# Which queue carries the first transposes and weight slabs of a fused SiLU MLP, and when each is issued

## The chip, the cores and the metric

The kernel runs on one core of a Trainium2 chip. The core has a matrix engine (TensorE, PE in the profile, with its weight loads shown as PEld), three other compute engines (VectorE or DVE, ScalarE or ACT, GpSimd or POOL), and SyncE (SP), which here only issues DMAs. SyncE and ScalarE each own one DMA queue; both queues feed the same 16 DMA engines. The metric is the device time of one execution in microseconds; lower is better. A profile comes from one further execution, with its own time.

## What is computed

The reference is a two-layer perceptron without biases, in bf16, on 2048 tokens:

```python
B, S, D, F = 1, 2048, 640, 1728
def reference(x, w1, w2):
    h = jnp.einsum("bsd,df->bsf", x, w1)
    h = jax.nn.silu(h)
    return jnp.einsum("bsf,fd->bsd", h, w2)
```

## The kernel before

Both layers contract over the partition axis of SBUF, so x is needed with its 640 columns on partitions. The kernel gets it so by transposing DMAs from HBM: the tensor `xT` has five tiles of 128 columns (index k, "tile k" below, DT = 5), each holding all 2048 tokens. `turned(c0, c1, k0, k1)` (lines 89 to 94) issues on SyncE one such DMA for tokens c0 to c1 and tiles k0 to k1. The first layer's weights are in `w1s`, again five slabs k of 128 rows; `slab(eng, k, f0, f1)` (line 118) loads the feature tiles f0 to f1 of slab k on the queue of `eng`. Every such DMA has a semaphore of its own, which stands at 16 once it has landed; `load` and `turned` return it as a point that an engine can be made to wait for.

The tokens go in four chunks of 512 (SCH). The first chunk is done in a special order, the opening: since weights and inputs arrive slab by slab, TensorE takes slab k=0 for eight feature tiles (NO = 8, one PSUM bank each), then k=1 for the same eight, and so on to k=4, after which ScalarE applies SiLU and writes `hT`. One feature tile of one k is a pair of matmuls (`step`, line 179), each with 64 of the 128 weight columns and 512 tokens, that run side by side. `sweep(k, ...)` waits for slab k and tile k and issues the eight pairs. Remaining feature tiles and chunks follow with all five k in a row, then the second layer, whose results are stored by SyncE, and the last of them by ScalarE too.

Before the first real matmul TensorE runs dummies on a zeroed tile `z` (`dummies`, line 129; `first_dummies`, line 135): thirteen matmuls of 128 weight columns and 256 columns of zeros, and then one pair with 64 weight columns each. They write PSUM bank 3, which the opening then starts anew.

A program begins with a barrier of all engines. `early(emit, engine, arrived)` (line 98) moves the instructions that `emit` makes ahead of it: for SyncE, ScalarE and VectorE (`arrived=False`) ahead of the engine's own arrival at the barrier, so that the barrier opens for nobody before these are issued; for TensorE (the opening, k = 0 to 2) behind its arrival but ahead of its wait. What follows in program order on an engine (SyncE's further loads, ScalarE's table load for SiLU at line 153, TensorE's k=3 and on) comes after the barrier.

Each engine's queue is in program order. The DMAs ahead of the barrier are issued before the change as follows:

| queue | order of issue before |
|---|---|
| SyncE | tiles 0 and 1; slab 0, feature tiles 5 to 7 (`ld_w1b`); slab 1; slab 2; tile 2; slab 3; tiles 3 and 4; slab 4 |
| ScalarE | slab 0, feature tiles 0 to 4 (NA = 5) |

After the barrier SyncE issues the rest of `w1s` (two DMAs), the fifteen one-tile transposes of chunks 1 to 3 (line 159) and `w2`.

What TensorE waits for in the opening: k=0 for `ld_t[0]` and `ld_w1[0]`, its sixth feature tile for `ld_w1b`, and each later k for `ld_w1[k]` and `ld_t[k]`. Where two names hold the same point, the second wait is left out by `wait` (line 63).

Of the kernel before, what the change touches and what calls it, by code (L numbers as in the profile page):

```python
# [9 lines left out]
def bass_standalone__dense_activation_silu__prompt_kernel(  # L10
# [13 lines left out]
    P = 128  # L24
    NB = 8
    BANK = 512
    DT = D // P
    FT = F // P
    FL = F - FT * P
    SCH = 512  # L30
    HB = 256
# [7 lines left out]
    pe, act, dve, pool, sp = nc.tensor, nc.scalar, nc.vector, nc.gpsimd, nc.sync  # L39

    with ExitStack() as es:
        def sb(name, shape, dtype):
            return es.enter_context(nc.sbuf_tensor(name, shape, dtype))
# [10 lines left out]
        z = sb("z", [P, HB], bf16)  # L54
        ps = es.enter_context(nc.psum_tensor("ps", [P, NB, BANK], fp32))
# [4 lines left out]
        def sem(name):  # L60
            s = es.enter_context(nc.semaphore(name))
            count[s.name if hasattr(s, "name") else name] = 0
            return [s, 0]

        def tick(ins, s, n=1):
            ins.then_inc(s[0], n)
            s[1] += n
            return (s, s[1])

        def wait(eng, *points):  # L70
            for pt in points:
                if pt is None:
                    continue
                s, v = pt
                key = (id(eng), id(s))
                if seen.get(key, 0) < v:
                    eng.wait_ge(s[0], v)
                    seen[key] = v

        s_pe, s_act, s_dve = sem("s_pe"), sem("s_act"), sem("s_dve")  # L80
# [4 lines left out]
        def load(eng, out_ap, in_ap):  # L85
            s = sem(f"s_ld{n_dma[0]}")
            n_dma[0] += 1
            return tick(eng.dma_start(out=out_ap, in_=in_ap), s, 16)

        def turned(c0, c1, k0, k1):  # L90
            s = sem(f"s_tr{n_dma[0]}")
            n_dma[0] += 1
            return tick(sp.dma_start_transpose(
                out=xT[:, k0:k1, c0:c1], in_=xf[c0:c1, k0 * P:k1 * P]), s, 16)

        ET = mybir.EngineType

        def early(emit, engine, arrived=True):
            n = len(nc.main_func.blocks[0].instructions)
            r = emit()  # L100
            lst = nc.main_func.blocks[0].instructions
            new = lst[n:]
            del lst[n:]
            at = next(
                i for i, ins in enumerate(lst)
                if ins.opcode == ("EventSemaphore" if arrived else "Drain") and ins.engine == engine
            )
            lst[at:at] = new
            return r
# [4 lines left out]
        NO = NB  # L114
        NA = 5
        CO = NO * P

        def slab(eng, k, f0=0, f1=NO):
            return load(eng, w1s[:, k, f0 * P:f1 * P], w1_v[:, k, f0 * P:f1 * P])

        ld_w1 = {}
        ld_t = {}
        ld_t[0] = ld_t[1] = early(lambda: turned(0, SCH, 0, 2), ET.SP, False)
        ld_w1[0] = early(lambda: slab(act, 0, 0, NA), ET.Activation, False)
        p_z = early(lambda: tick(dve.memset(z[:, :], 0.0), s_dve), ET.DVE, False)  # L125

# [2 lines left out]
        def dummies(n, w):  # L129
            for _ in range(n):  # L130
                for c0 in range(0, P, w):
                    pe.matmul(ps[c0:c0 + w, 3, 0:HB], lhsT=z[:, 0:w], rhs=z[:, :],  # L132
                              start=True, stop=True)

        def first_dummies():
            wait(pe, p_z)
            dummies(13, P)
            dummies(1, HC)

        p_warm = tick(pool.memset(warm[:, :], 0.0), s_pool)  # L140

        ld_w1b = early(lambda: slab(sp, 0, NA, NO), ET.SP, False)
        ld_w1[1] = early(lambda: slab(sp, 1), ET.SP, False)
        ld_w1[2] = early(lambda: slab(sp, 2), ET.SP, False)
        ld_t[2] = early(lambda: turned(0, SCH, 2, 3), ET.SP, False)
        ld_w1[3] = early(lambda: slab(sp, 3), ET.SP, False)
        ld_t[3] = ld_t[4] = early(lambda: turned(0, SCH, 3, DT), ET.SP, False)
        ld_w1[4] = early(lambda: slab(sp, 4), ET.SP, False)
        CM = CO + 2 * P
        ld_rest = load(sp, w1s[:, :, CO:CM], w1_v[:, :, CO:CM])  # L150
        ld_rest2 = load(sp, w1s[:, :, CM:F], w1_v[:, :, CM:F])
        wait(act, p_warm)
# [17 lines left out]
        def mm(o, l, r, start, stop, shared=False):  # L170
            return pe.matmul(o, lhsT=l, rhs=r, start=start, stop=stop, skip_group_check=shared)  # L171
# [7 lines left out]
        def step(b, k, ft, c0, c1, start=False, stop=False):  # L179
            for h0 in (0, HC):  # L180
                ins = mm(ps[h0:h0 + HC, b, :], w1s[:, k, ft * P + h0:ft * P + h0 + HC],
                         xT[:, k, c0:c1], start, stop, shared=True)
            return ins
# [9 lines left out]
        def opening():  # L193
            first_dummies()
            wait(pe, ld_t[0], ld_w1[0])
            for ft in range(NO):
                if ft == NA:
                    wait(pe, ld_w1b)
                part(0, ft, 0, SCH, start=True)
            for k in (1, 2):  # L200
                sweep(k, 0, SCH, ld_w1[k], ld_t[k])
# [11 lines left out]
        def bank():  # L213
            b = nxt[0] % NB
            nxt[0] += 1
            wait(pe, bank_free[b])
            return b

        wait(pe, ld_rest)
        for ft in range(NO, FT):  # L220
            b = bank()
            if ft == NO + 2:
                wait(pe, ld_rest2)
            for k in range(DT):
                ins = step(b, k, ft, 0, SCH, start=(k == 0), stop=(k == DT - 1))
            silu(hT[:, ft, 0:SCH], ps[:, b, :], b, tick(ins, s_pe))
        for c in range(1, NSC):
            wait(pe, ld_xc[c])
            for ft in range(FT):
                b = bank()  # L230
                for k in range(DT):
                    ins = step(b, k, ft, c * SCH, (c + 1) * SCH, start=(k == 0), stop=(k == DT - 1))
                h_last = silu(hT[:, ft, c * SCH:(c + 1) * SCH], ps[:, b, :], b, tick(ins, s_pe))
        h_tail = []
        for q in range(NSC // 2):
            b = bank()
            for k in range(DT):
                for hh in range(2):
                    c = 2 * q + hh
                    ins = mm(ps[hh * FL:(hh + 1) * FL, b, :], w1s[:, k, F0:F],  # L240
                             xT[:, k, c * SCH:(c + 1) * SCH],
                             start=(k == 0), stop=(k == DT - 1), shared=True)
# [133 lines left out]
        for u, eng in ((A, dve), (B, act), (C, act), (E, dve), (G2, act)):  # L376
            for ft in range(FT):
                ins = u.whole(ft, ft == FT - 1)
# [31 lines left out]
```

## Time and profile before

| what | value |
|---|---|
| median of three runs | 124.61 us (124.58, 124.61, 125.4) |
| the profiled execution's own time | 124.91 us |
| its span, first to last instruction | 123.4 us |
| TensorE busy in the span | 121.1 us, 98% |
| ScalarE, VectorE busy | 38.8 us, 7.0 us |
| dummies (line 132) | 15 matmuls, 3.3 us |
| first-layer matmuls (line 171, from xT and w1s) | 540, 59.2 us, 382 ns mean |
| DMA: bytes moved, mean rate | 10.42 MB, 84 GB/s |

The span runs from the first to the last instruction; the run's time also has what lies around it, 1.5 us here. A matmul's 382 ns is its time from start to end; the two of a pair and the pairs among themselves overlap, so the pace is read from starts, not from this. A DMA issue shows on the queue of its engine as SPq or ACTq; its length there is the time to issue, and "to landing" counts from the start of the issue to the last of its semaphore's sixteen steps. Times in the timeline are microseconds from the start of the span. In the windows view each column is an engine's busy time with the number of its instructions, and the last columns are the granted clock, the DMA engines' mean busy share (over 1 where packets of an engine overlap) and their rate.

### The profile page before, as it was taken

The page shows a single profiled execution, that of the slowest core. Times are in us where ns is not written, and L with a number is a line of the kernel's source. Part 1 is how long each engine was busy: PE and PEld are TensorE (multiplying, and loading weights), DVE is VectorE, ACT ScalarE, POOL GpSimd, SP SyncE. Part 2 cuts the span into 40 slices and gives each one's busy share as a digit, 9 for nine tenths or more (in the row PEclk, how much of TensorE's full clock was granted, in tenths as well). Part 3 has the DMA queues.
Part 4 walks back from the last instruction along what each step waited for, and adds up shares of the span by engine and source line. Part 5 has one row for each costly group of instructions (what it writes and reads, how often), then busy time and mean ns, then how long its engine had stood idle before and what let it go on. Part 6 is the DMA issues. An engine that isn't in the chain of part 4 may idle for free.

```text
span 123.4 us, 2299 instructions
## 1 busy us (share of the span) xinstructions
PE 121.1 (98%) x1057; PEld 59.5 (48%) x1057; DVE 7.0 (6%) x11; ACT 38.8 (31%) x67; POOL 0.3 (0%) x5
## 2 busy tenths in 40 slices
PE   8999999999999999999999999999999999999993
PEld 5455555555555555555544444444444444444452
DVE  0000000000000000000000022002201300222001
ACT  0041985555555555555530011001101200110110
POOL 0000000000000000000000000000000000000000
PEclk9999999999999999999999999999999999999999
DMA  6999945475992000000000005202200220022112
GB/s 142 234 271 302 157 103 108 94 75 92 288 391 70 0 0 0 8 0 0 0 0 5 0 5 115 56 0 106 106 0 5 106 106 0 5 106 106 53 74 86
DMA packets 19482, 10.42 MB, mean 84 GB/s; under 512 B 13457, under 2 KB 18961, under 8 KB 19473
## 3 DMA queue, kind: packets, MB, share of 16 engines
q1 hardware_dynamic: 19184, 10.05, 32.1%
q10 hardware_dynamic: 288, 0.23, 0.8%
q8 instruction: 8, 0.13, 0.5%
q14 instruction: 2, 0.01, 0.0%
HBM read 4.51 MB, written 2.62 MB: 58 GB/s over the span
## 4 chain that ended last, share of the span: by engine, by line
PE 95%; DMA 3%; ACT 0%; issue 0%
PE ps L171 95%; DMA xT<-in_x_dram 3%; ACT o_sb L254 0%
## 5 line engine op out<-in xcount | busy, mean ns | idle before, releaser
L171 PE MATMUL ps<-xT,w1s 128*64 128x512 bf16 x540 | 59.2, 382 | 0.1
L171 PE MATMUL ps<-w2s,hT 64*128 64x512 bf16 (+3 forms) x377 | 46.2, 369 | 0.0
L171 PEld LDWEIGHTS ps<-xT,w1s 128*64 128x64 bf16 x540 | 30.5, 111 | 28.6 <-issue 0.9
L175 ACT ACTIVATE hT<-ps 128x512 bf16<-128x512 f32 x52 | 30.0, 607 | 22.9 <-PE ps L171 22.9
L171 PEld LDWEIGHTS ps<-w2s,hT 64*128 64x128 bf16 (+1 forms) x377 | 21.0, 95 | 24.1 <-issue 0.2
L254 ACT CAST o_sb<-ps 128x512 bf16<-128x512 f32 (+1 forms) x9 | 5.0, 551 | 41.5 <-PE ps L171 41.5
L171 PE MATMUL ps<-hT,w2s 64*128 64x512 bf16 x104 | 11.7, 376 | 0.0
L171 PEld LDWEIGHTS ps<-hT,w2s 64*128 64x128 bf16 x104 | 5.0, 94 | 6.3 <-issue 0.4
L252 DVE CAST o_sb<-ps 128x512 bf16<-128x512 f32 (+1 forms) x8 | 5.4, 675 | 40.5 <-PE ps L171 40.5
L252 DVE CAST oT<-ps 128x512 bf16<-128x512 f32 x2 | 1.4, 692 | 73.8 <-PE ps L171 73.8
L254 ACT CAST oT<-ps 128x512 bf16<-128x512 f32 x2 | 1.2, 586 | 10.6 <-PE ps L171 10.6
L132 PE MATMUL ps<-z 128*128 128x256 bf16 (+1 forms) x15 | 3.3, 419 | 0.4 <-DVE z L125 0.4
L153 ACT ACT_TABLE_LOAD x1 | 1.3, 1283 | 7.1 <-DVEq L395 7.1
L171 PE MATMUL ps<-w2t,hTt 64*128 64x512 bf16 (+2 forms) x17 | 2.9, 363 | 0.0
L132 PEld LDWEIGHTS ps<-z 128*128 128x128 bf16 (+1 forms) x15 | 1.9, 142 | 1.5 <-issue 0.4
L175 ACT ACTIVATE hTt<-ps 128x512 bf16<-128x512 f32 x2 | 1.2, 597 | 1.0 <-PE ps L171 1.0
L171 PEld LDWEIGHTS ps<-w2t,hTt 64*128 64x128 bf16 x17 | 0.9, 94 | 1.1
L171 PE MATMUL ps<-hTt,w2t 64*128 64x512 bf16 x4 | 0.8, 376 | 0.0
L171 PEld LDWEIGHTS ps<-hTt,w2t 64*128 64x128 bf16 x4 | 0.2, 94 | 0.2
L153 ACT ACTIVATE warm<-warm 128x32 f32<-128x32 f32 x1 | 0.2, 229 | 0.0
L125 DVE MEMSET z<- 128x128 uint32 x1 | 0.2, 165 | 0.2 <-issue 0.2
L140 POOL MEMSET warm<- 128x32 f32 x1 | 0.1, 125 | 6.7 <-POOLq L395 6.7
(4 smaller groups left out, 0.4 us busy)
## 6 DMA issues: line engine op xcount, KB each, us to landing
out_dram<-o_sb SPq DMA_DIRECT2D x15, 160.0 KB, 1.8
w2s<-in_w_dram SPq DMA_DIRECT2D x1, 1120.0 KB, 6.1
w1s<-in_w_dram SPq DMA_DIRECT2D x4, 256.0 KB, 3.9
w2s<-in_w_dram SPq DMA_DIRECT2D x1, 960.0 KB, 8.4
w1s<-in_w_dram SPq DMA_DIRECT2D x1, 560.0 KB, 5.5
w1s<-in_w_dram SPq DMA_DIRECT2D x1, 320.0 KB, 4.3
xT<-in_x_dram SPq DMA_TRANSPOSE x18, 3.9
w1s<-in_w_dram ACTq DMA_DIRECT2D x1, 160.0 KB, 2.7
```

What stands on the lines that cost most here:

```text
L125: p_z = early(lambda: tick(dve.memset(z[:, :], 0.0), s_dve), ET.DVE, False)
L132: pe.matmul(ps[c0:c0 + w, 3, 0:HB], lhsT=z[:, 0:w], rhs=z[:, :], start=True, stop=True)
L140: p_warm = tick(pool.memset(warm[:, :], 0.0), s_pool)
L153: act.activation(out=warm[:, :], in_=warm[:, :], func=ACT.Silu)
L171: return pe.matmul(o, lhsT=l, rhs=r, start=start, stop=stop, skip_group_check=shared)
L175: r = tick(act.activation(out=out_ap, in_=in_ap, func=ACT.Silu), s_act)
L252: r = tick(dve.tensor_copy(out=out_ap, in_=in_ap), s_dve)
L254: r = tick(act.copy(out=out_ap, in_=in_ap), s_act)
```

## The change

The transposes of the first chunk are cut 1, 2, 2 instead of 2, 1, 2 and become the first three instructions of SyncE's queue, with slabs 3 and 4 behind them. Slab 0's second part and slabs 1 and 2 go to ScalarE's queue. There the first two wait for the fourth dummy, which counts up TensorE's semaphore `s_pe` as its first step (`gate`), and slab 2 waits for the landing of the second transpose, tiles 1 and 2. The dummies become 4 and 6 and one pair instead of 13 and one pair. Nothing else differs.

| queue | order of issue after |
|---|---|
| SyncE | tile 0; tiles 1 and 2; tiles 3 and 4; slab 3; slab 4 |
| ScalarE | slab 0, feature tiles 0 to 4; wait for the fourth dummy; slab 0, feature tiles 5 to 7; slab 1; wait for tiles 1 and 2; slab 2 |

```diff
-        ld_t[0] = ld_t[1] = early(lambda: turned(0, SCH, 0, 2), ET.SP, False)
+        ld_t[0] = early(lambda: turned(0, SCH, 0, 1), ET.SP, False)
         ld_w1[0] = early(lambda: slab(act, 0, 0, NA), ET.Activation, False)
...
         def dummies(n, w):
             for _ in range(n):
                 for c0 in range(0, P, w):
-                    pe.matmul(ps[c0:c0 + w, 3, 0:HB], lhsT=z[:, 0:w], rhs=z[:, :],
-                              start=True, stop=True)
+                    ins = pe.matmul(ps[c0:c0 + w, 3, 0:HB], lhsT=z[:, 0:w], rhs=z[:, :],
+                                    start=True, stop=True)
+            return ins
+
+        gate = (s_pe, 1)

         def first_dummies():
             wait(pe, p_z)
-            dummies(13, P)
+            assert tick(dummies(4, P), s_pe) == gate
+            dummies(6, P)
             dummies(1, HC)
...
-        ld_w1b = early(lambda: slab(sp, 0, NA, NO), ET.SP, False)
-        ld_w1[1] = early(lambda: slab(sp, 1), ET.SP, False)
-        ld_w1[2] = early(lambda: slab(sp, 2), ET.SP, False)
-        ld_t[2] = early(lambda: turned(0, SCH, 2, 3), ET.SP, False)
+        ld_t[1] = ld_t[2] = early(lambda: turned(0, SCH, 1, 3), ET.SP, False)
+        ld_t[3] = ld_t[4] = early(lambda: turned(0, SCH, 3, DT), ET.SP, False)
         ld_w1[3] = early(lambda: slab(sp, 3), ET.SP, False)
-        ld_t[3] = ld_t[4] = early(lambda: turned(0, SCH, 3, DT), ET.SP, False)
         ld_w1[4] = early(lambda: slab(sp, 4), ET.SP, False)
+
+        def held():
+            wait(act, gate)
+            b, n1 = slab(act, 0, NA, NO), slab(act, 1)
+            wait(act, ld_t[1])
+            return b, n1, slab(act, 2)
+
+        ld_w1b, ld_w1[1], ld_w1[2] = early(held, ET.Activation, False)
```

## The prediction

> **What bounds the kernel now.** I read the totals and the chain on the page, then the timeline of the first microseconds, then the DMA view cut so narrow that each answer holds one issue, then the load on the DMA engines per microsecond.
>
> The page's totals, and its chain that ended last:
>
> ```profile
> PE 121.1 (98%) x1057; PEld 59.5 (48%) x1057; DVE 7.0 (6%) x11; ACT 38.8 (31%) x67; POOL 0.3 (0%) x5
> ...
> PE 95%; DMA 3%; ACT 0%; issue 0%
> ```
>
> The same chain in order of time (start, length, what):
>
> ```profile
> 0.00 3.72 DMA xT<-in_x_dram
> 3.72 0.04 issue
> 3.76 117.77 PE ps L171 x1041
> ```
>
> TensorE never waits again after 3.76, so the change can gain only ahead of that point, and can lose wherever it opens a hole later. The timeline (start, length, engine, line, operation):
>
> ```profile
> 0.00 1.33 SPq L93 DMA_TRANSPOSE xT<-in_x_dram  x1
> 0.12 0.40 ACTq L88 DMA_DIRECT2D w1s<-in_w_dram  x1
> ...
> 0.39 3.31 PE L132 MATMUL ps<-z 128*128 128x256 bf16 x15 [0.39 <-DVE z L125]
> 1.38 1.58 SPq L88 DMA_DIRECT2D w1s<-in_w_dram  x3
> 3.01 1.15 SPq L93 DMA_TRANSPOSE xT<-in_x_dram  x1
> 3.27 0.13 PEld L132 LDWEIGHTS ps<-z 128*64 128x64 bf16 x2 [0.41 <-issue]
> 3.76 0.18 PEld L171 LDWEIGHTS ps<-xT,w1s 128*64 128x64 bf16 x4 [0.36 <-DMA xT<-in_x_dram]
> ...
> 4.62 0.18 PEld L171 LDWEIGHTS ps<-xT,w1s 128*64 128x64 bf16 x2 [0.25 <-issue]
> ...
> 5.05 0.18 PEld L171 LDWEIGHTS ps<-xT,w1s 128*64 128x64 bf16 x2 [0.25 <-issue]
> 5.42 16.52 PEld L171 LDWEIGHTS ps<-xT,w1s 128*64 128x64 bf16 x154 [0.19 <-issue]
> ```
>
> Two things to see. The first transpose is the last to arrive, behind dummies that are over. And the pitch of the pairs (two 64-column matmuls side by side) is 4.62 to 5.05 = 0.43 us at first; later ScalarE starts a feature tile of five pairs at 18.79 and the next at 19.87, so 1.08/5 = 0.216 each. The pair from 5.05 to 5.42 takes 0.37, between the two, which puts the doubling at about 5.36. (The granted-clock column reads 1.00 in every slice here, so speed is read from the pitch.) Laying pairs from there, k=0 runs 3.76 to 6.28, k=1 to 8.01, k=2 to 9.73, k=3 to 11.46; ScalarE's first SiLU at 11.88 fits. I use 8.01, the start of k=2, as the yardstick: it shifts the end one for one while PE stays dense.
>
> Landings: issue's start plus the DMA view's time to landing gives slab 0's five tiles at 0.12+2.7 = 2.8, transposes 0 and 1 at 3.7, slab 0's rest at 1.38+3.8 = 5.2 (the three issues from 1.38 are some 0.53 apart), slab 1 at 2.0+3.8 = 5.8 (needed 6.28), slab 2 at 2.5+4.0 = 6.5, transpose 2 at 3.01+4.1 = 7.1 (needed 8.01), slab 3 at 7.9, transposes 3 and 4 at 8.9 (needed 9.73), slab 4 at 10.5 (needed 11.46). Nothing has a whole microsecond to spare. The DMA engines are full meanwhile (last two columns: share, GB/s):
>
> ```profile
> 3.00:4.00 1.00, 0.93 (x6) 0.31 (x6) 0.00 (x0) 0.00 (x0) 0.00 (x0) 1.00 0.77 121
> 4.00:5.00 1.00, 1.00 (x6) 0.36 (x4) 0.00 (x0) 0.00 (x0) 0.00 (x0) 1.00 0.92 307
> 5.00:6.00 1.00, 1.00 (x10) 0.52 (x8) 0.00 (x0) 0.00 (x0) 0.00 (x0) 1.00 1.29 288
> 6.00:7.00 1.00, 1.00 (x14) 0.52 (x10) 0.00 (x0) 0.00 (x0) 0.00 (x0) 1.00 0.97 232
> 7.00:8.00 1.00, 1.00 (x12) 0.49 (x10) 0.00 (x0) 0.91 (x1) 0.12 (x1) 1.00 1.16 285
> 8.00:9.00 1.00, 1.00 (x12) 0.56 (x10) 0.00 (x0) 0.60 (x2) 0.00 (x0) 1.00 1.14 287
> ```
>
> **First transpose alone.** It carries 131 KB less. At 257 GB/s (the slice 2 to 3, when transposes alone moved) that is 0.51 us. Its issue is also shorter: the one-tile issue at 3.01 took 1.15, the two-tile one at 4.82 took 1.24, so 0.09. Landing 3.72-0.60 = 3.1. Bounds: 2.8, the issue-to-landing time of a lone one-tile transpose at 17.3, and 3.72. I take 3.1, built from this very transfer.
>
> **Three dummies fewer.** Dummies follow each other every 0.213 us (256 columns). They end streaming at about 3.27+0.22 = 3.49 now, so at 2.85 then; the data still come last. TensorE starts k=0 at 3.15 instead of 3.76: 0.61 us of work at half speed, worth 0.61/0.43 = 1.4 pairs, or 1.4 x 0.216 = **0.31 us** at the end, as long as the speed doubles at 5.36 again. Bounds 0 and 0.47 (starts at 3.76 and 2.83). Pairs laid from 3.15: slab 0's rest is needed at 5.28, k=1 at 5.95, k=2 at 7.68, k=3 at 9.40, k=4 at 11.13.
>
> **The gate and ScalarE's queue.** The fourth dummy starts at 1.0 and lasts 0.42; its count costs TensorE nothing that the dummies don't hide. ScalarE issues slab 0's rest from 1.45 to about 1.95 and slab 1 to 2.5 (0.40 to 0.58 each in the rows). Landing by rows 2.7 to 3.8 after issue: 4.2 to 5.2 for the rest (need 5.28), 4.7 to 5.8 for slab 1 (need 5.95). Just in time, no cost; without that cover, up to some 0.3.
>
> **Second transpose, tiles 1 and 2.** Issued from about 1.29 to 2.53. Below: 1.29+2.8 and 0.5 for the second tile's bytes, 4.6. Above: today slab 1 lands at 5.8 with transposes 0 and 1 and slab 0 ahead; with tile 2's 131 KB more at 273 GB/s (mean of the slices from 5 to 9) the whole set is in at 6.3. I take 5.5, short of the upper end, since the two queues together should fill the 0.77 hole of the slice 3 to 4. Need 5.95.
>
> **Slab 2, held by it.** This is the added wait that counts. Behind it on ScalarE stand only slab 2's issue, the start-up barrier and the table load. Issue at 5.55, and landing 2.7 later by the ScalarE row, which had the engines nearly to itself: **8.25**. A second way: it lands at 6.5 today; now transpose 2 and transposes 3 and 4 go ahead of it (the latter are queued on SyncE's ring from 3.8, and slab 2 needs a landing and an issue to get going), 393 KB at 273 GB/s, 1.44 us, giving 8.0; and slab 3, next on SyncE's ring, may take up to half of the engines, 262 KB or 0.96 us more, less the hole filled. Both ways say 8.0 to 8.9. Bounds: 4.6+2.7 = 7.3 and 6.3+0.05+3.8 = 10.1 (other slabs' rows, which include a queue). I take 8.25, and so k=2 starts at 8.3 instead of 8.01: **+0.3 us**, though TensorE was 0.33 ahead when it ran dry at 7.68.
>
> A rule bears on the sharing. The Trainium skill ("DMA: Bandwidth & Descriptors", "Issuing engines are not separate DMA queues") says that transfers of all issuers run on the same 16 engines and interleave, and that a second issuer saves issue time alone. By that rule slab 2 pays the whole 0.96, lands near 9, and the sum is +1.0 (rival 2 has the same from rows); the trace shows both queues moving packets between 1.9 and 2.4, but not two slabs against each other.
>
> **Moved past the rest.** SyncE loses three issues (1.58 us), and tile 2 rides with tile 1: its five early issues end at about 5.1 instead of 6.7, ScalarE's at 6.0. The barrier goes from 7.09 to some 6.4, so table load, later transposes and remaining weights start 0.7 earlier. Worth nothing: the first SiLU isn't due before 11.5, and k=3 and k=4 have data by 9 and 10.
>
> **Sum.** The profiled execution took 124.91 (span 123.4 and 1.5 around it); +0.3 gives **125.2**. The runs' median is 124.61, fastest 124.58. They can be lower because k=2 may start as early as slab 1's landing allows, 5.8+8 x 0.216 = 7.55, if the speed doubles sooner, which would be 124.45. A wait for slab 2 doesn't depend on that, so 125.2 stands as the new median too.
>
> **Rivals.**
> 1. *All arrives in time* (0.22): second transpose at 4.6 to 4.9, slab 2 by 7.7. Then 124.91-0.31 = 124.6, in runs that double early down to 124.2. For: TensorE's first wait does fall. Against: slab 2's chain of three latencies.
> 2. *Slab 2 much later* (0.14): the second transpose itself lands near 6.3 or slab 3 shares fully; k=2 at 9.0 to 9.3, 125.9 to 126.2. Decides once slab 2 lands after 8.9.
> 3. *The speed doubles later* (0.08): it came 4.97 us after the first dummy. If the gap before the real work restarts that count at 3.15, doubling comes at 8.12; 11.6 pairs are then done, k=2 starts at 9.07, 125.97. Against: today's gap is as long. The Trainium skill ("TensorE: Matmul & The Clock Gate", "What's actually happening") has a free-running activity window of about 3.4 us; by it a missed window would cost 1.7 us (an estimate).
> 4. *The first transpose isn't earlier* (0.06), because its latency and not its bytes set 3.72: start as now, slab 2 late as forecast, 125.2 to 125.4.
>
> Forecast 0.50. A change under 1% (1.25 us) is about what a measurement of this kernel can't tell from none. Faster by more, below 123.36, would need k=2 at 8.01-1.55 = 6.46, which leaves k=1 no time after slab 1's landing: 0.02. Slower by more needs 125.86: rival 2, most of 3, the forecast's edge: 0.22. Within: 0.76. The range 124.2 to 126.2 runs from rival 1's lower end to rival 2's upper.
>
> **What would show it.** The wait before the first L171 pair ends near 3.1; a second idle of TensorE of 0.3 to 1 us on a DMA into w1s, 16 pairs later; ScalarE's third slab issue near 5.5; the table load before 7.09. No second idle and the first SiLU before 11.6 means rival 1. Pairs still 0.43 apart after 6 mean rival 3.

## The result, and the profile after

The change makes the kernel slower: 127.94 us (median of six runs, 127.14 to 129.13) against 124.62 before, a ratio of 1.0245 with a 95% interval of 1.020 to 1.029. The forecast was 125.2 with a range from 124.2 to 126.2. (The ratios here and below leave out executions more than 1.5% above the fastest of their kernel, so they are not quite the quotients of the medians.) The profiled execution took 127.66 (span 126.2), 2.75 more than the one of before.

The chain of the changed kernel in order of time (start, length, what):

```profile
0.00 1.23 SPq L93
...
1.29 6.59 DMA xT<-in_x_dram
...
7.90 2.79 DMA w1s<-in_w_dram
...
10.73 102.17 PE ps L180 x944
```

Before, TensorE was the chain from 3.76 on. Now the second transpose holds it until 7.88 and slab 2 until 10.68. The timeline has the same from TensorE's side:

```profile
3.19 0.19 PEld L180 LDWEIGHTS ps<-xT,w1s 128*64 128x64 bf16 x4 [0.43 <-DMA xT<-in_x_dram]
...
5.76 0.18 PEld L180 LDWEIGHTS ps<-xT,w1s 128*64 128x64 bf16 x2 [0.24 <-issue]
7.98 1.47 PEld L180 LDWEIGHTS ps<-xT,w1s 128*64 128x64 bf16 x16 [2.04 <-DMA w1s<-in_w_dram]
...
10.72 5.32 PEld L180 LDWEIGHTS ps<-xT,w1s 128*64 128x64 bf16 x52 [1.28 <-DMA w1s<-in_w_dram]
```

k=0 starts at 3.2, as intended. Then there are two holes, ahead of k=1 and ahead of k=2. (The first is put down to w1s, since the releaser is inferred; the chain has the transpose, which landed 0.2 after slab 1, at 7.65. Without the transpose, slab 1 would have held k=1 almost as long.) k=2 starts at 10.73 instead of 8.01: 2.72 later, and that is the whole of the 2.75. Why the transpose is late shows in the load of the DMA engines (last two columns: share, GB/s):

```profile
4.00:5.00 1.00, 1.00 (x8) 0.46 (x6) 0.00 (x0) 0.00 (x0) 0.00 (x0) 1.00 1.36 197
5.00:6.00 1.00, 1.00 (x8) 0.45 (x6) 0.00 (x0) 0.00 (x0) 0.00 (x0) 1.00 0.78 79
6.00:7.00 1.00, 0.82 (x4) 0.00 (x0) 0.00 (x0) 0.00 (x0) 0.00 (x0) 1.00 1.22 213
7.00:8.00 1.00, 0.00 (x0) 0.02 (x1) 0.00 (x0) 0.00 (x0) 0.00 (x0) 1.00 1.18 216
```

Over these four microseconds the engines' share is about what it was (1.14 in the mean, 1.09 before), but they move 176 GB/s instead of 278. From 5 to 6 the rate is 79 instead of 288. The share is lower in that slice, but not in the same slice of a second trace of the changed kernel ("change again" below):

```profile
5.00:6.00 1.00, 1.00 (x10) 0.33 (x6) 0.00 (x0) 0.00 (x0) 0.00 (x0) 1.00 1.16 95
```

Busy time is not bytes.

### The profile page after: what moved, and what is told of

It reads as the page before. It is cut to its first block, busy times and chain, and to the rows that moved or that the text cites. A ratio compares the mean times of both kernels' runs of the same rounds, so it can differ in the third digit from the quotient of the medians.

```text
span 126.2 us, 2292 instructions
## 1 busy us (share of the span) xinstructions
PE 121.6 (96%) x1053; PEld 59.5 (47%) x1054; DVE 6.9 (6%) x11; ACT 38.8 (31%) x67; POOL 0.3 (0%) x5
## 4 chain that ended last, share of the span: by engine, by line
PE 90%; DMA 7%; SPq 1%; issue 0%; ACT 0%
PE ps L180 90%; DMA xT<-in_x_dram 5%; DMA w1s<-in_w_dram 2%; SPq L93 1%; ACT o_sb L263 0%
## 5 line engine op out<-in xcount | busy, mean ns | idle before, releaser
L180 PE MATMUL ps<-xT,w1s 128*64 128x512 bf16 x540 | 60.6, 387 | 2.1 <-DMA xT<-in_x_dram 1.2
L180 PEld LDWEIGHTS ps<-xT,w1s 128*64 128x64 bf16 x540 | 31.0, 112 | 31.5 <-DMA w1s<-in_w_dram 3.3
L132 PE MATMUL ps<-z 128*128 128x256 bf16 (+1 forms) x12 | 2.7, 419 | 0.4 <-DVE z L125 0.4
```

The lines of the kernel that those rows point to most:

```text
L132: ins = pe.matmul(ps[c0:c0 + w, 3, 0:HB], lhsT=z[:, 0:w], rhs=z[:, :], start=True, stop=True)
```

## The experiments

Each kernel was timed beside before on the same chip; before's median was 124.3 to 125.0. "From issue" is the second transpose's time from the start of its issue to landing, as the chain or the DMA view has it.

| kernel | median us | ratio (95%) | second transpose lands, from issue |
|---|---|---|---|
| change, first result | 127.94 | 1.0245 (1.020 to 1.029) | 7.9, 6.6 |
| change again | 128.12 | 1.026 (1.020 to 1.032) | 8.15, 6.9 |
| change, third time | 128.38 | 1.031 (1.025 to 1.037) | 7.3, 6.0 |
| no wait for slab 2 | 125.89 | 1.011 (1.005 to 1.017) | 6.15, 4.9 |
| the same again | 128.84 | 1.029 (1.022 to 1.037) | 9.0, 7.7 |
| filler, with the wait | 127.94 | 1.023 (1.017 to 1.028) | 9.6, 8.3 |
| filler, no wait | 126.87 | 1.018 (1.012 to 1.023) | 8.3, 7.0 |
| second transpose without copies beside it | 131.15 (one run) | | 5.3, 4.0 |
| copies beside copies | 126.41 (one run) | | 7.6, 5.2 |
| one queue, 1-2-2 | 125.30 | 1.008 (1.006 to 1.010) | 6.1, 3.7 |
| one queue, slabs 2 and 3 together | 125.30 | 1.004 (1.002 to 1.007) | 6.35, 3.9 |
| one queue, single tiles | 125.87 | 1.010 (1.007 to 1.013) | |
| one queue, tile 0 then tile 1 | 126.58 | 1.013 (1.009 to 1.016) | |
| two queues, no cut, no wait | 126.15 | 1.014 (1.008 to 1.020) | |
| before, traced again | 125.31 (one run) | | |

My theory after this result was **mixing**: a transpose in flight on one queue and a copy on the other slow each other far below what either reaches alone. The rivals were **volume** (bytes and place set the landing, whatever the queue), **two queues** (any two busy queues disturb each other), and that slab 2's wait did the damage.

**One queue.** Everything but slab 0's first part goes back to SyncE:

```diff
+        ld_w1b = early(lambda: slab(sp, 0, NA, NO), ET.SP, False)
+        ld_w1[1] = early(lambda: slab(sp, 1), ET.SP, False)
         ld_t[1] = ld_t[2] = early(lambda: turned(0, SCH, 1, 3), ET.SP, False)
+        ld_w1[2] = early(lambda: slab(sp, 2), ET.SP, False)
         ld_t[3] = ld_t[4] = early(lambda: turned(0, SCH, 3, DT), ET.SP, False)
         ld_w1[3] = early(lambda: slab(sp, 3), ET.SP, False)
         ld_w1[4] = early(lambda: slab(sp, 4), ET.SP, False)
-        def held():
...
-        ld_w1b, ld_w1[1], ld_w1[2] = early(held, ET.Activation, False)
```

> The cut 1, 2, 2 and the ten dummies of the change, but all slabs save slab 0's first part back on SyncE's queue: tile 0; slab 0's rest; slab 1; tiles 1 and 2; slab 2; tiles 3 and 4; slab 3; slab 4. No transpose is in flight beside a copy of the other queue, save slab 0's first part. Theory 'mixing' (a transpose and a copy on different queues slow each other): the second transpose lands at 6.0 to 6.6 instead of 7.9, k=1 starts by 6.7, time 124.3 to 125.0. Rival 'volume' (the bytes ahead and the two-tile cut set it, whatever the queue): it lands at 7.3 or later, time 126.5 or more. Rival 'two queues' (any two busy queues slow each other) expects what 'mixing' does here.

The transpose landed at 6.1, with the same slabs ahead of it that run beside it in the change, and most of the loss is gone. That speaks against volume. The time is 0.3 over what was expected: TensorE starts at 2.94 and then stops three times, the last time for slab 3, which lands at 10.4 (7.9 before).

**The transpose without copies beside it.** Slab 0's rest goes ahead, slab 1 waits as slab 2 does:

```diff
-            wait(act, gate)
-            b, n1 = slab(act, 0, NA, NO), slab(act, 1)
+            b = slab(act, 0, NA, NO)
             wait(act, ld_t[1])
-            return b, n1, slab(act, 2)
+            return b, slab(act, 1), slab(act, 2)
```

> As the change, but slab 0's rest is issued at once behind its first part and slab 1 as well as slab 2 waits for the second transpose, so that this one has the engines almost to itself. Mixing: the second transpose lands at 4.6 to 5.2; slab 1 then runs beside tiles 3 and 4 and lands after 8.5; time over 126. If the two-tile transpose behind another transpose is slow by itself, it still lands after 7. Volume: about 5.5.

```profile
1.29 3.98 DMA xT<-in_x_dram
```

This is the line of its chain that answers to "1.29 6.59" above: same transfer, same place in SyncE's queue, 2.6 us less. The transpose isn't slow by itself. (It is a little over the expected 5.2; tile 0, with slab 0's rest beside it now, came only at 4.04.) The kernel as a whole is the slowest of all, for another reason that comes below.

**Copies beside copies.** ScalarE's queue as in the change up to slab 1, but SyncE has slabs 2 and 3 at that time:

```diff
+        ld_w1[2] = early(lambda: slab(sp, 2), ET.SP, False)
+        ld_w1[3] = early(lambda: slab(sp, 3), ET.SP, False)
         ld_t[1] = ld_t[2] = early(lambda: turned(0, SCH, 1, 3), ET.SP, False)
         ld_t[3] = ld_t[4] = early(lambda: turned(0, SCH, 3, DT), ET.SP, False)
-        ld_w1[3] = early(lambda: slab(sp, 3), ET.SP, False)
...
-            wait(act, ld_t[1])
-            return b, n1, slab(act, 2)
+            return b, n1
```

> ScalarE's queue has slab 0's rest and slab 1 behind the gate as in the change, but beside them SyncE's has copies: tile 0; slab 2; slab 3; tiles 1 and 2; tiles 3 and 4; slab 4. Slab 2 is held by nothing. Mixing: slabs 0 to 3 have all landed by 6.0 to 6.5 at 280 GB/s or more from 4 to 5, the second transpose at 7.0 to 7.5, time 125.0 to 126.0. Two queues: copies slow each other as well, slabs 1 to 3 land after 7, the rate from 4 to 6 stays under 220 GB/s, time over 127.

From 4.0 to 5.5 the DMA view of this kernel (packets and bytes; then each queue's bytes and its share of the 16 engines' time) says:

```profile
DMA packets 329, 0.56 MB, mean 372 GB/s; under 512 B 41, under 2 KB 67, under 8 KB 329
...
q10 hardware_dynamic: 164, 0.26, 51.8%
q1 hardware_dynamic: 165, 0.29, 51.6%
```

and that of the change, run again, from 4.5 to 7.0:

```profile
DMA packets 727, 0.37 MB, mean 147 GB/s; under 512 B 624, under 2 KB 624, under 8 KB 727
...
q1 hardware_dynamic: 619, 0.16, 65.5%
q10 hardware_dynamic: 108, 0.21, 52.0%
```

In both, the two queues share the engines about evenly. With copies on both (q1 is SyncE's, q10 ScalarE's) they move 372 GB/s, with transposes on one of them (the many packets under 512 B) 147. The theory of two queues falls. Packet times say the same. My estimate from these lines (share times 16 engines times the window, over packets) gives 76 ns for a packet of ScalarE's queue beside copies and 193 ns beside transposes. (They hold 1.6 and 1.9 KB in the mean.) It gives 42 ns for one of SyncE's transposes there, against 24 ns where they had the engines nearly to themselves (the first view under "No wait for slab 2"). So both kinds take about twice as long; it isn't only that a transpose's packets are small.

The time missed its range by 0.4: the slabs were in by 6.7, the second transpose behind them at 7.6, and k=2 started at 9.46, 1.45 later than before.

**No wait for slab 2.** `wait(act, ld_t[1])` is taken out, so slab 2 follows slab 1 at once; run on two chips.

> As the change, without slab 2's wait for the second transpose: it is issued right behind slab 1. Mixing: slab 2 mixes too, so the second transpose lands no earlier than 7.9, at 8 to 9, and slab 2 by 9.5; k=2 waits little; time 126.2 to 127.2. If the wait alone were the loss, the second transpose lands as forecast near 5.5 to 6.3 and the time is 125.2 or less.

> The changed kernel as it is, once more, beside the next one on the same chip. Theory 'chain' (slab 2 lands 2.8 after the second transpose, and the transpose itself is late by an amount that differs from execution to execution): in this trace slab 2 lands 2.7 to 2.9 after the second transpose wherever that lands, and k=2 starts right there; time = 124.9 + (start of k=2 - 8.0) within 0.3. Theory 'mixing' (transpose and copies on two queues always slow each other): the second transpose lands at 7.5 or later again, with a microsecond under 100 GB/s between 4 and 7.

> The change without slab 2's wait, once more, beside the change itself. Chain: the wait's price is what the change has more than this kernel, 1.2 to 2.2 us on the medians, since slab 2 lands within 1 us behind slab 1; the second transpose lands at 6 to 8 here too. Mixing: the second transpose lands at 7.5 or later, as in the change, and the difference of the two is under 1 us.

On the first chip the median was 125.89, but the traced execution, 124.95, was its best, with the transpose in at 6.15, which speaks against "always". Its DMA view, 3.0 to 4.6 and then 4.6 to 5.9, shows why:

```profile
q1 hardware_dynamic: 952, 0.24, 88.4%
q10 hardware_dynamic: 66, 0.07, 14.7%
```

```profile
q10 hardware_dynamic: 232, 0.44, 100.2%
q1 hardware_dynamic: 64, 0.01, 4.2%
```

Here the queues happened to take turns: nearly all transposes first, then copies at 347 GB/s. Two queues with the same contents cost far less when their packets don't interleave: this execution is 0.6 above before's median on that chip. On the second chip they did interleave, the transpose landed at 9.0, and the kernel was no faster than the change beside it. So "always" is to be dropped from the theory: of seven traces with this layout six landed at 7.3 to 9.6 and one at 6.15. What decides between the two courses stays open.

Before was traced once more as well, to see whether its landings are as uneven. I expected 0.5 us or more of difference if they were, and a time within 0.5 of 124.6 all the same. They are not: slab 1 came at 5.6 and tile 2 at 6.9, each within 0.25 of the first trace. But the time was 125.31, outside that, since the pairs stayed 0.43 apart until 6.23 and not 5.36, and k=2 started at 8.40:

```profile
5.81 0.18 PEld L171 LDWEIGHTS ps<-xT,w1s 128*64 128x64 bf16 x2 [0.24 <-issue]
6.23 8.76 PEld L171 LDWEIGHTS ps<-xT,w1s 128*64 128x64 bf16 x82 [0.24 <-issue]
```

So the moment of full speed differs between executions of one kernel. Read from the pitch of the pairs, it lies between 3.3 and 6.6 in the thirteen traces in which TensorE had no idle of a microsecond ahead of k=0 and reached full speed within k=0 or at its end.

The chain theory's other half held: slab 2 landed 2.8, 2.8 and 2.7 us after the transpose in the three traces of the change. But in the second trace k=2 did not start there, and the windows show something new (third column from the right: granted clock):

```profile
7.00:8.00 1.00, 0.00 (x0) 0.00 (x0) 0.00 (x0) 0.00 (x0) 0.00 (x0) 1.00 1.29 228
8.00:9.00 1.00, 0.71 (x6) 0.48 (x8) 0.00 (x0) 0.07 (x1) 0.07 (x1) 0.74 1.15 373
9.00:10.00 1.00, 1.00 (x8) 0.62 (x6) 0.00 (x0) 1.00 (x1) 0.05 (x1) 0.50 1.05 346
10.00:11.00 1.00, 1.00 (x7) 0.50 (x5) 0.00 (x0) 0.44 (x2) 0.00 (x0) 0.50 0.89 252
11.00:12.00 1.00, 1.00 (x8) 0.56 (x6) 0.00 (x0) 0.00 (x0) 0.00 (x0) 0.55 0.99 239
```

TensorE had reached full speed in k=0 and idled for 2.7 us by its weight loads (2.3 by the matmuls' rows, whose ends are modelled). From about 8.48 (0.74 of that slice) to 11.9 (0.55 of that one) the clock is at half. k=1 then takes 3.2 us, 1.5 more than at full speed, and k=2 starts at 11.49, so slab 2, in at 11.0, is no longer waited for. A late transpose is paid a second time, by 1.5 us through the clock here, by 1.0 through slab 2's wait in the first trace. The two don't add up, since one hides the other.

The runs' mean clocks tell how much of the loss this is. Of the fourteen executions of the change on three chips, six have a mean clock of 0.987, which is some 3.4 us at half speed; they took 128.41 to 129.47, median 129.0. The eight at full clock took 126.98 to 128.17, median 127.6. So the clock costs some 1.4 us where it falls, and the larger part, some 3 us over before, is there without it.

**Filler.** Sixteen more dummies between k=0 and k=1 keep TensorE busy. They add zeros to open banks, so the sums are unchanged:

```diff
+            for i in range(16):
+                pe.matmul(ps[:, i % NB, 0:HB], lhsT=z[:, 0:P], rhs=z[:, :],
+                          start=False, stop=False, skip_group_check=True)
             for k in (1, 2):
                 sweep(k, 0, SCH, ld_w1[k], ld_t[k])
```

> The change again, as the measure for the two kernels with filler on the same chip: 127.5 to 128.6, the second transpose at 7.5 to 8.5.

> The change with sixteen more dummies between k=0 and k=1; they add zeros to the eight open banks and run while TensorE would wait for the second transpose. Theory 'mixing, then the clock' (the late transpose costs 2 us by itself, and the gap it opens lets the clock fall back for 3.4 us in some executions): no execution has pairs at 0.43 after 8.5, the spread shrinks, the time is 127.0 to 127.7, at the change's fastest runs or below, since slab 2 is still 2.8 behind the transpose. If the clock had no part in it: 127.5 to 128.5, as the change.

> The same filler without slab 2's wait for the second transpose: the price of that wait with the clock held up. Mixing, then the clock: the second transpose lands at 7.5 to 9.0, slab 2 within 1 us of it, k=1 and k=2 run without a stop between, 126.0 to 127.2, and 0.5 to 1.3 less than with the wait. If the wait is free (what it costs slab 2 it gives the transpose): the same as with it, within 0.4.

By the mean granted clock, it didn't fall back in any of the eight executions with filler, but did in two of four of the change on the same chip (0.987). But the first expectation failed in its time: 127.94 is above its 127.0 to 127.7, where it was to be if the clock had no part, and the interval of the ratio overlaps the change's (1.025 to 1.037). The times still spread from 126.99 to 129.35; in the slowest, the one traced, the transpose itself came only at 9.6. The filler holds the clock up; that it makes the kernel faster is not shown. Without the wait the median is 1.07 lower, as expected, but the intervals of the two ratios overlap (1.017 to 1.028 and 1.012 to 1.023), and without filler the difference had the other sign. The price of slab 2's wait is therefore between nothing and some 1 us, and not settled.

**The cut by itself.** Two of the one-queue kernels ask whether starting with one tile pays once nothing is mixed. They differ from the first in SyncE's order alone: tile 0, slab 0's rest, slab 1, tile 1, slab 2, tile 2, slab 3, tiles 3 and 4, slab 4; and tile 0, slab 0's rest, slab 1, tiles 1 and 2, slabs 2 and 3, tiles 3 and 4, slab 4.

> The order of before on SyncE's queue, with the first two-tile transpose cut into tile 0 in front and tile 1 behind slab 1: tile 0; slab 0's rest; slab 1; tile 1; slab 2; tile 2; slab 3; tiles 3 and 4; slab 4; ten dummies. Bytes ahead of each slab are those of before, from tile 1 on. If the early start is worth what the prediction said, k=0 starts near 3.0, k=1 at 6.0 to 6.3 and the time is 0 to 0.3 below before. If one issue more on SyncE or the later tile 1 costs: k=1 starts at 6.5 or later, 0.2 to 0.8 above before.

> All on SyncE's queue, no more turns from transposes to copies than before the change has: tile 0; slab 0's rest; slab 1; tiles 1 and 2; slabs 2 and 3; tiles 3 and 4; slab 4; ten dummies. Theory 'turns' (each place where copies follow transposes in a queue costs some 0.5 us of the engines, which is why cutting the first transpose off didn't pay in the one-queue kernels): tile 0 at 3.0, the second transpose at 5.9 to 6.2, slab 3 at 8.2 to 8.7, the third at 9.0 to 9.6, time 124.0 to 124.7, within 0.3 of before. If the cut itself costs whatever the order: 125.0 to 126.0, as the two one-queue kernels.

Neither pays: 1.0% and 0.4% slower. In the first, TensorE starts at 3.14 and stops ahead of k=1, k=2 and k=3, the last time until the third transpose is in at 10.4 (9.0 before). In the second, slab 3 lands at 8.95 and the third transpose at 10.0, each later than expected and than before. My theory of turns (that each place where copies follow transposes costs the engines 0.5 us) is not borne out by these landings: turns were as many as before. TensorE, though, never stops in that execution:

```profile
0.00 3.26 DMA xT<-in_x_dram
...
3.31 118.66 PE ps L175 x1041
```

It starts 0.45 earlier than before and loses that and more at half speed, which lasts until about 6.6. k=2 starts at 8.40 and the time is 125.36, as in before's second trace, where full speed was late too. The landings would have cost nearly as much by themselves: with full speed at 5.36 it would have come to k=2 near 7.8 (my estimate), and slab 2 was in only at 8.26 (6.5 before). So here the one hides the other; which of them made the other nine executions slow isn't known.

**Cut and split, one at a time.** The last two start from before. The one cuts its first transpose in two, one behind the other, and has ten dummies instead of thirteen (not shown below); the other moves slabs 1 and 2 to ScalarE:

```diff
-        ld_t[0] = ld_t[1] = early(lambda: turned(0, SCH, 0, 2), ET.SP, False)
+        ld_t[0] = early(lambda: turned(0, SCH, 0, 1), ET.SP, False)
...
+        ld_t[1] = early(lambda: turned(0, SCH, 1, 2), ET.SP, False)
```

```diff
-            dummies(13, P)
+            assert tick(dummies(4, P), s_pe) == gate
+            dummies(9, P)
...
-        ld_w1[1] = early(lambda: slab(sp, 1), ET.SP, False)
-        ld_w1[2] = early(lambda: slab(sp, 2), ET.SP, False)
+        def held():
+            wait(act, gate)
+            return slab(act, 1), slab(act, 2)
+
+        ld_w1[1], ld_w1[2] = early(held, ET.Activation, False)
```

> Before, with nothing changed but that the first two-tile transpose is two of one tile, one right behind the other, and ten dummies: tile 0; tile 1; slab 0's rest; slab 1; slab 2; tile 2; slab 3; tiles 3 and 4; slab 4, one queue, no turn more than before. If the early start pays once neither mixing nor turns come with it: k=0 from 3.0 to 3.2, tile 1 at 3.8 to 4.2, slab 1 by 6.0, time 0.1 to 0.4 below before. If the issue more on SyncE makes every slab late by its 1.2 us: slab 1 at 6.4 or later, TensorE stops ahead of k=1, time 0 to 0.6 above before.

> Before, with slabs 1 and 2 alone moved to ScalarE's queue behind the fourth dummy: no cut, no wait for a transpose, thirteen dummies. Tile 2 is then issued at 2.0 and can be in flight beside slab 1. Mixing: a microsecond between 4 and 7 at under 200 GB/s, slab 1 or tile 2 at 6.3 or later (5.8 and 7.1 before, though tile 2 now has 0.5 MB less ahead of it), time 125.3 to 127.5. If the split of the queues is harmless by itself and the cut or the wait did the damage: tile 2 by 5.8, slab 1 by 5.8, time within 0.4 of before.

The split alone costs 1.4%, inside what mixing expected. Two windows of its trace, and the line of its chain that holds TensorE:

```profile
5.00:6.00 1.00, 0.45 (x6) 0.00 (x0) 0.00 (x0) 0.00 (x0) 0.00 (x0) 1.00 2.13 281
6.00:7.00 1.00, 0.17 (x2) 0.14 (x4) 0.00 (x0) 0.91 (x1) 0.12 (x1) 1.00 0.60 64
...
1.39 5.40 DMA w1s<-in_w_dram
```

The share over 2 is packets that lie on top of each other; then the engines move 64 GB/s from 6 to 7. TensorE stops in k=0 for slab 0's rest, which lands at 6.8 instead of 5.2. Slab 1 landed at 6.6 instead of 5.8, and tile 2 at 7.9 instead of 7.1 though 0.5 MB less stood ahead of it. Neither the cut nor slab 2's wait is needed for a loss. But this trace doesn't show transposes of one queue against copies of the other: from 6 to 7 only 12 of the 165 packets are ScalarE's, with 5% of the engines' time, and what runs together there is slab 0's rest and tile 2, both in SyncE's queue. Transposes and copies can meet within a queue too, where the copies ahead are late.

The cut, with three dummies fewer, costs 1.3%, though not by late slabs: slab 1 came at 6.35, near the expected 6.4, but TensorE was done with k=0 only at 7.4. Its timeline:

```profile
3.98 0.19 PEld L176 LDWEIGHTS ps<-xT,w1s 128*64 128x64 bf16 x4 [1.21 <-DMA xT<-in_x_dram]
...
8.25 0.18 PEld L176 LDWEIGHTS ps<-xT,w1s 128*64 128x64 bf16 x2 [0.25 <-issue]
8.62 6.37 PEld L176 LDWEIGHTS ps<-xT,w1s 128*64 128x64 bf16 x60 [0.19 <-issue]
```

Most of tile 0 landed from 3.04, but its last part at 3.93. With three dummies fewer TensorE idled 1.2 us ahead of it, and full speed came near 8.5 rather than at 5.4, outside the 3.3 to 6.6 of the traces without such an idle. Some 3.2 us more at half speed are 1.6 us, which is about the loss in this execution. That the idle delayed full speed is likely, but no run varies it alone. Whether the other five had the same cause isn't known, since only one was traced.

No kernel tried is faster than the one before.

## Why the prediction was wrong

**First transpose, dummies, early start.** Right in size: landing 3.15 (forecast 3.1), first real pair at 3.19 (3.15). Its worth of 0.31 us never appeared, because TensorE only came sooner to data that weren't there. In the one-queue kernels, too, an earlier start ended in later stops in two of the three traces, and in the third at half speed that lasted longer. The prediction had 0.45 us of slack for the second transpose and 0.15 for slab 1 at the late end of its range, and treated that as enough; and its 0.31 needed full speed at 5.36 again, which two traces of before already don't agree on.

**Gate and ScalarE's queue.** Slab 0's rest landed at 4.6, inside its 4.2 to 5.2. Slab 1 came at 7.65, outside its 4.7 to 5.8: the rows it was priced from had no transposes on the other queue. It would have held k=1 by itself until then, so the same missing price struck here too.

**Second transpose.** This is the step that failed. It was put at 5.5 with 4.6 and 6.3 as bounds, and came at 7.9 (7.3 to 9.6 in six of seven traces of this layout). Even the upper bound took the 273 GB/s of one queue in order for both queues together; I even counted on the second queue to fill a hole. The runs show 79 to 213 GB/s from 4 to 7 while transposes and copies interleave; why they slow each other stays open. The only row of before with both queues at work was from 1.9 to 2.4, where slab 0's first part had 18% of the engines' time beside the first transpose; it was too little to show a price. The trace of before had no price for two full queues at once, so I should have bounded the rate from below with far less than that of one.

**The rule on interleaving.** The Trainium skill ("DMA: Bandwidth & Descriptors", "Issuing engines are not separate DMA queues") was used for slab 2 against slab 3, where it didn't matter: slab 2 landed 2.8 after its issue, near the 2.7 I took. It speaks of shared engines that interleave, and I read that as a conserved rate. For two streams of copies such a rate agrees with the trace (372 GB/s), for transposes against copies it doesn't (147).

**Slab 2's wait.** The mechanism and its 2.7 us were right, and in the first trace it made the second hole, 1.0 us after k=1. What it costs beyond a late transpose is unsettled, as said.

**Rivals.** Rival 2 named the right event, a late second transpose, and was priced too low, at 125.9 to 126.2, since it stopped at a landing of 6.3. Rival 3, the clock, was given 0.08. Its own sign came true, for the pairs of k=0 were 0.43 apart to their end, past 6. But before's second trace, with thirteen dummies, has that until 6.23, so a changed gap isn't needed for it; and it cost nothing here, since k=1's data came only at 7.9. Half speed that did cost came later, in two of the change's first six runs by their mean clock. In the one trace of the change that caught it, its second, the clock fell after the hole behind k=0.

**Moved past the rest.** The barrier opened at 8.65, not at 6.4, since ScalarE stood in its wait. As forecast that was free: the table load ended at 9.9 and the first SiLU came at 14.6.

## What to carry to other kernels

Don't put DMA transposes on one queue and copies on another so that they are in flight together, unless a trace shows them taking turns; keep them in one queue, or hold the copies until the transposes have landed (if the matrix engine doesn't run dry meanwhile: the kernel that held two slabs was the slowest here), and price any new overlap from a row that has that overlap, not from the rate of one queue. Where the data arrive just in time, starting the matrix engine earlier gains nothing unless every later landing moves too. And a hole in the first microseconds can cost again through the clock, so I would remove dummies only where the data come surely.

## What the hardware showed unexpectedly

With a transpose and slab copies on two queues the 16 DMA engines moved 79 GB/s in one whole microsecond, and 95 at a share of 1.16 in another trace, against 362 to 372 with copies on both and 347 when the two took turns. Why isn't known.

The clock fell to half for 3.4 us after TensorE had idled 2.7 us (by the weight loads' rows). The Trainium skill ("TensorE: Matmul & The Clock Gate", "Why this matters for your kernels") warns of gaps over about 3 us; here less was enough. In the change's first and third trace, gaps of 2.0 and 1.8 us left the clock up. The 3.4 us agree with the window length that the page gives under "What's actually happening". In the kernel where the transpose ran without copies TensorE stood idle for 1.3 us ahead of k=0 and for 2.9 ahead of k=1, and its pairs were still 0.43 apart at 14.9, which by my estimate is 3.6 of the 6.2 us that kernel took more than before.

The clock column reads 1.00 during the first, slow microseconds in all traces; the pitch of the pairs is the surer reading there. By it full speed came at 5.36 in one trace of before and at 6.23 in the other, which alone moves k=2 by 0.4 us.
